# The first 17 and the last 4 microseconds of a fused attention and MLP kernel: transfers, LayerNorm and clock warm-up rearranged, last output tile cut in three

## Chip, cores, metric

One core of a Trainium2 chip. The metric is the device time of one execution in microseconds, taken over several executions. Six engines appear in the profile: PE (TensorE matmuls), PEld (its weight loads), DVE (VectorE), ACT (ScalarE), POOL (GpSimd), SP (SyncE, which here only issues transfers).

## The reference, cut to what matters

```python
mod = (silu(c) @ w_mod).reshape(1, 6, 1, 512)         # c: 512 values, w_mod: 512 x 3072
sa, ca, ga, sb, cb, gb = mod[:, 0], ..., mod[:, 5]
h = layernorm(x) * (1 + ca) + sa                      # x: 2048 x 512
x = x + ga * attention(h @ wq, k_cache[-512:], v_cache[-512:]) @ wo   # 32 heads of 128
h = layernorm(x) * (1 + cb) + sb
x = x + gb * (relu(h @ w1) @ w2)                      # 512 -> 1792 -> 512
```

All inputs and the output are bf16. Before the first query projection can run, four things must be there: the first 512 rows of x normalized and transposed, SiLU of c, its product with two sixths of w_mod (the "modulation columns"), and the first heads of wq.

## The kernel before

The rows of x are dealt so that partition p holds rows 16p to 16p+15; a tile is one row of each partition, and the first block of 512 rows is four tiles. The opening, in program order (cuts marked; `kb.op(engine, ...)` appends to that engine's stream and works out its semaphore waits from `reads` and `writes`):

```python
dma(c_col[:, :], c[0].rearrange("(c p) -> p c", p=P), "c", writes=[R_c], eng=ACT)
for t in range(TPB):                                   # TPB = 4 tiles
    dma(x_sb[:, t, :], xv[:, t, :], f"xa{t}", writes=[R_x[t]], eng=ACT if t % 2 else SP)
load_wm(1)                                             # two sixths of w_mod, SyncE queue
load_wm(0)
load_wq(0, 2); load_k(0); load_v(0); load_wq(2, 2)
# ... memsets, identity matrix, ScalarE's table ...
warm(48)                       # 48 matmuls of ident x ident, 128 columns, result unused
ln_stat(0); ln_stat(1); silu() # statistics on VectorE; silu: exp on ScalarE, rest on VectorE
ln_stat(2); ln_rstd(0, 0, 3); ln_stat(3); ln_rstd(0, 3, 4)   # power -0.5 on GpSimd
for tl in range(3):
    ln_norm(tl)                # VectorE
    ln_tposes(tl, [0, 2])      # four 128x128 transposes on TensorE into PSUM
for f in mod_cols_mm(0, QBK): f()   # 32 matmuls of one column
ln_norm(3); ln_tposes(3, [0, 2])
mod_cols_evac(0, QBK)
ln_mod_ps([0, 2], hT[0], R_hT[0], 1)   # scale and shift, two columns on DVE, two on ACT
# ...
q_mms(0); q_mms(1, 5)          # first query projections: 4 matmuls of 512 columns each
```

The end of each output tile (`y_group`): 14 matmuls of 512 columns, then two VectorE operations and a store.

```python
for fc in range(FC):           # FC = 14
    mm(bank[bk], h1T[b % 2][:, fc, tl*P:(tl+1)*P], w2_sb[:, fc, :], ...)
kb.op(DVE, lambda e: e.tensor_tensor(yt[i], bank[bk], gbf[:, :], op=ALU.mult), ...)
kb.op(DVE, lambda e: e.tensor_tensor(yo[i], yt[i], x_sb[:, t, :], op=ALU.add), ...)
dma(ov[:, t, :], yo[i], f"y{i}", reads=[R_yo[i]])
```

## Time and profile before

| | before |
|---|---|
| time, median of three (later four) executions | 568.4 us (568.33 of four, 567.71 to 568.82) |
| span of the profiled execution | 566.1 us |
| TensorE busy | 557.6 us, 98% |
| four tiles of x landed | 3.07, 5.28, 4.67, 6.95 us |
| modulation weights landed | 7.85 and 9.36 us |
| first query projection starts | 12.44 us |
| first exponential of scores starts | 16.88 us |
| last matmul ends, span ends | 562.43, 566.14 us |

Times inside an execution are microseconds from the span's start. A transfer has landed when its semaphore has its last count in the trace. The row to watch is the first exponential of scores: from there on the kernel is a steady pipeline that no part of the change touches. So "first exponential" measures the opening, and "last matmul to end of span" measures the end. The trace also records the clock that TensorE is granted: here it is 0.50 (half speed) from 9.85 to 16.68 us and 1.00 after. Below, "released" means that it goes to full speed, and it "falls" when it goes back to half. A "wide" matmul has 512 columns.

### The profile page before, as it was taken

What the parts mean: (1) busy time and instruction counts of PE and PEld (TensorE: products, weight loads), DVE (VectorE), ACT (ScalarE), POOL (GpSimd) and SP (SyncE); (2) the same over time, 40 slices, a digit from 0 to 9 for tenths busy, and PEclk for the clock granted to TensorE, in tenths of its full rate; (3) what the DMA queues carried; (4) which work ended last, traced back from release to release, by engine and by line L of the source; (5) the groups of instructions that cost most, each with busy time, mean ns of one, the idle gap of its engine ahead of it and who ended that gap; (6) DMA issues with size and microseconds to landing.
All of it is one profiled execution on the core that took longest, in us unless ns stands there. A gap on an engine that the chain in (4) does not pass through costs nothing.

```text
span 566.1 us, 9753 instructions
## 1 busy us (share of the span) xinstructions
PE 557.6 (98%) x4169; PEld 318.8 (56%) x4169; DVE 242.8 (43%) x532; ACT 347.5 (61%) x445; POOL 38.7 (7%) x41
## 2 busy tenths in 40 slices
PE   6999999999999999999999999999999999999997
PEld 5565555555565555555555555555555654444443
DVE  4344465533333655333346553333354448322133
ACT  2876666666666666666666666666666644432500
POOL 1000000002300000033000000330000000000000
PEclk8999999999999999999999999999999999999999
DMA  9785768342232147242522532121224210200001
GB/s 225 204 194 120 179 127 172 75 80 41 41 75 39 37 76 149 41 110 45 143 54 59 91 59 39 38 38 38 40 41 73 44 30 1 47 29 22 22 28 47
DMA packets 114340, 42.67 MB, mean 75 GB/s; under 512 B 94192, under 2 KB 113904, under 8 KB 114288
## 3 DMA queue, kind: packets, MB, share of 16 engines
q1 hardware_dynamic: 113472, 41.70, 35.1%
q8 instruction: 34, 0.56, 0.4%
q10 hardware_dynamic: 816, 0.26, 0.2%
q14 instruction: 18, 0.15, 0.1%
HBM read 18.35 MB, written 2.10 MB: 36 GB/s over the span
## 4 chain that ended last, share of the span: by engine, by line
PE 98%; DVE 1%; DMA 1%; issue 0%; ACTq 0%
PE psS L1351 28%; PE psO L1351 26%; PE psQ L1351 23%; PE psW L1351 20%; DMA x<-in_A_x_dram 1%; DVE st L1361 0%; PE psS L1354 0%; DVE PT L1632 0%; DVE PT L1633 0%; DVE mv L1362 0%; DVE hT L1398 0%; ACTq L1296 0%; DVE xn L1372 0%; DVE rstd L1366 0%; DVE tmp L1410 0%
## 5 line engine op out<-in xcount | busy, mean ns | idle before, releaser
L1465 ACT ACTIVATE PT<-psS 128x1024 bf16<-128x1024 f32 x256 | 262.7, 1028 | 129.6 <-PE psS L1351 129.6
L1351 PE MATMUL psS<-qT,kT 128*128 128x512 bf16 x512 | 152.2, 380 | 0.0
L1351 PEld LDWEIGHTS psO<-v,PT 128*128 128x128 bf16 x2048 | 126.6, 98 | 30.2
L1351 PE MATMUL psO<-v,PT 128*128 128x129 bf16 x2048 | 137.0, 220 | 0.0
L1351 PE MATMUL psQ<-hT,wq 128*128 128x512 bf16 x508 | 131.2, 381 | 0.8 <-DVE hT L1398 0.8
L1351 PE MATMUL psW<-wo,oT 128*128 128x512 bf16 x512 | 130.6, 379 | 0.0
L1475 DVE RECIPROCAL rinv<-psO 128x4 f32<-128x4 f32 x128 | 23.3, 182 | 234.9 <-PE psO L1351 234.9
L1476 DVE TENSOR_TENSOR o<-psO,rinv 128x512 bf16<-128x512 f32 x128 | 88.5, 691 | 4.7 <-DVE rinv L1475 0.3
L1351 PEld LDWEIGHTS psQ<-hT,wq 128*128 128x128 bf16 x508 | 49.8, 98 | 61.4 <-issue 1.5
L1351 PEld LDWEIGHTS psS<-qT,kT 128*128 128x128 bf16 x512 | 49.8, 98 | 59.5 <-ACT PT L1465 0.7
L1457 ACT ACTIVATE qT<-psQ 128x512 bf16<-128x512 f32 x127 | 75.2, 592 | 1.2 <-PE psQ L1351 1.2
L1621 ACT ACTIVATE wq<-psS 128x512 bf16<-128x512 f32 x56 | 33.4, 597 | 49.5 <-PE psS L1351 49.5
L1351 PEld LDWEIGHTS psW<-wo,oT 128*128 128x128 bf16 x512 | 45.0, 98 | 32.9 <-DVE acc L1498 1.2
L1498 DVE TENSOR_TENSOR acc<-psW,acc 128x512 f32<-128x512 f32 x48 | 33.1, 690 | 6.7 <-PE psW L1351 6.7
L1351 PE MATMUL psO<-wmw,wq 128*128 128x512 bf16 x140 | 31.2, 379 | 0.0
L1367 POOL TENSOR_TENSOR rstd<-rstd,cst 128x4 f32<-128x4 f32 (+2 forms) x9 | 8.7, 962 | 273.4 <-DVE rstd L1366 273.3
L1501 POOL TENSOR_TENSOR acc<-acc,gaf 128x512 f32<-128x512 f32 x12 | 15.3, 1271 | 168.7 <-DVE acc L1498 168.7
L1351 PE MATMUL psS<-h2T,wmw 128*128 128x512 bf16 x112 | 25.3, 379 | 0.0
L1351 PE MATMUL psS<-hT,wmw 128*128 128x512 bf16 x112 | 24.5, 379 | 0.0
L1632 DVE TENSOR_TENSOR PT<-psO,gbf 128x512 f32<-128x512 f32 x10 | 6.9, 691 | 40.2 <-PE psO L1351 40.2
L1361 DVE BATCH_NORM_STATS2 st<-x 128x6 f32<-128x512 bf16 x32 | 21.7, 679 | 4.4 <-DMA x<-in_A_x_dram 4.4
L1351 PEld LDWEIGHTS psO<-wmw,wq 128*128 128x128 bf16 x140 | 13.7, 98 | 16.5
(60 smaller groups left out, 168.9 us busy)
## 6 DMA issues: line engine op xcount, KB each, us to landing
wo<-in_A_wo_dram SPq DMA_DIRECT2D x4, 1024.0 KB, 6.1
wq<-in_A_wq_dram SPq DMA_DIRECT2D x7, 512.0 KB, 5.5
wmw<-in_B_w_dram SPq DMA_DIRECT2D x14, 256.0 KB, 3.1
wmw<-in_w_mod_dram SPq DMA_DIRECT2D x6, 512.0 KB, 5.5
oT<-o SPq DMA_TRANSPOSE x128, 2.4
out_dram<-PT SPq DMA_DIRECT2D x16, 128.0 KB, 1.8
x<-in_A_x_dram SPq DMA_DIRECT2D x3, 512.0 KB, 4.2
v<-in_A_v_cache_dram SPq DMA_DIRECT2D x8, 128.0 KB, 4.6
```

The costliest lines, as they stand in the source:

```text
L1351: kb.op(PE, lambda e: e.matmul(out_ap, lhsT, rhs, start=start, stop=stop), reads=reads, group_writes=[R_b[k] for k in bk], signal=signal)
L1361: kb.op(DVE, lambda e: e.bn_stats(st[:, t, :], x_sb[:, t, :]), reads=[R_x[t]], writes=[R_st[t]])
L1367: kb.op(POOL, lambda e: e.tensor_tensor(rstd[:, sl], rstd[:, sl], cst[:, 0:1].to_broadcast([P, hi - lo]), op=ALU.pow), reads=R_rstd[sl] + ...
L1457: kb.op(ACT, lambda e: e.activation(qT[u % NQT][:, :], bank[bk], ACTF.Copy), reads=[R_b[bk]], writes=[R_qT[u % NQT]])
L1465: kb.op(ACT, lambda e: e.activation(PT[u % NPT][:, pr * 2:pr * 2 + 2, :], s_ps[pr][:, :, :], ACTF.Exp, scale=scale), reads=[R_b[pr * 2], R ...
L1475: kb.op(DVE, lambda e: e.reciprocal(rinv[:, u, :], o_ps[:, :, P]), reads=[R_b[5], R_b[6]], writes=[R_rinv])
L1476: kb.op(DVE, lambda e: e.tensor_tensor(o_sb[u % NOS][:, :, :], o_ps[:, :, 0:P], rinv[:, u, :].unsqueeze(2).to_broadcast([P, TPB, P]), op=A ...
L1498: kb.op(DVE, lambda e: e.tensor_tensor(acc[:, tl, :], bank[WBK], acc[:, tl, :], op=ALU.add), reads=[R_b[WBK], R_acc[tl]], writes=[R_acc[tl]])
L1501: kb.op(eng, lambda e: e.tensor_tensor(acc[:, tl, :], acc[:, tl, :], gaf[:, :], op=ALU.mult), reads=[R_acc[tl], R_ga], writes=[R_acc[tl]])
L1621: kb.op(ACT, lambda e: e.activation(h1T[b % 2][:, fc, :], bank[bk], ACTF.Relu), reads=[R_b[bk]], writes=[R_h1[b % 2][fc]], pre=all_events( ...
L1632: kb.op(DVE, lambda e: e.tensor_tensor(yt[i], bank[bk], gbf[:, :], op=ALU.mult), reads=[R_b[bk], R_gb], writes=[R_yt[i]], pre=pt_done if c ...
```

## The change

The intent: get x, c and the modulation weights in faster, shorten VectorE's serial chain by giving one tile to ScalarE, keep TensorE's clock up through the first projections, and shorten what follows the last matmul. The core of the diff:

```diff
-    dma(c_col[:, :], c[0].rearrange("(c p) -> p c", p=P), "c", writes=[R_c], eng=ACT)
-    for t in range(TPB):
-        dma(x_sb[:, t, :], xv[:, t, :], f"xa{t}", writes=[R_x[t]], eng=ACT if t % 2 else SP)
-    load_wm(1)
-    load_wm(0)
-    load_wq(0, 2)
+    for i in range(2):                  # two transfers of 256 KB, rows of 2 KB
+        dma(x_sb[:, 2*i:2*i+2, :], xv[:, 2*i:2*i+2, :], f"xa{i}", ..., eng=ACT if i else SP)
+    dma(c_row[:, :], c[0].rearrange("(c p) -> c p", p=P), "c", writes=[R_c])   # 4 rows
+    load_wm01(0)                        # both sixths together: rows of 2 KB,
+    load_wm01(1, ACT)                   # half of the rows on each queue
+    load_wq(0, 2, ACT)
 # warm(n):
-            mm(bank[WBK][:, :P], ident[:, :], ident[:, :], ...)
+            mm(bank[WBK], ones[:, :], ones[:, 0:1].to_broadcast([P, QB]), ...)   # 512 columns
-    warm(48)
+    warm(7)
+    silu_exp(5)                         # c transposed on TensorE, exponential on ScalarE
+    warm(9)
+    # tile 3 on ScalarE: Copy with sum, Copy (-mean), Square with sum, Identity (+eps),
+    # after GpSimd's power: Copy (-mean*rstd), Identity with scale and bias
...
-    silu()
     ln_stat(2)
...
+    silu_mul(5)
     for tl in range(3):
         ln_norm(tl)
-        ln_tposes(tl, [0, 2])
-    for f in mod_cols_mm(0, QBK):
-        f()
-    ln_norm(3)
-    ln_tposes(3, [0, 2])
-    mod_cols_evac(0, QBK)
+    # first half of the modulation columns, transposes of tile 0, second half, copied out
+    for tl in range(1, TPB):
+        ln_tposes(tl, [0, 2])
+        warm(tl)                        # 1, 2, 3 wide matmuls
 # the last output tile:
+    mlp.pop()
+    mlp.extend(lambda a=a: y_group(NB - 1, TPB - 1, *a)
+               for a in ((0, D // 2, ACT), (D // 2, 3 * D // 4, SP), (3 * D // 4, D, ACT)))
```

With the last part go four output buffers in place of two.

More of the change, by code (lines that the diff above doesn't have):

```diff
@@ L1244, in build_fast @@
     wmw = T("wmw", [P, max(6 * DC * D, DC * F + FC * D)])
-    wm = [wmw[:, i * DC * D:(i + 1) * DC * D].rearrange("p (c n) -> p c n", c=DC) for i in range(6)]
+    wm01 = wmw[:, 0:2 * DC * D].rearrange("p (c n) -> p c n", c=DC)
+    wm = [wm01[:, :, 0:D], wm01[:, :, D:2 * D]] + [wmw[:, i * DC * D:(i + 1) * DC * D].rearrange("p (c n) -> p c n", c=DC) for i in range(2, 6)]
     w1_sb = wmw[:, 0:DC * F].rearrange("p (c f) -> p c f", c=DC)
@@ L1249, in build_fast @@
     xnT = T("xnT", [P, TPB, DC, P])
-    NY = 2
-    yt = [PT[0][:, :, :].rearrange("p a b -> p (a b)")[:, 2 * i * D:2 * (i + 1) * D].bitcast(F32) for i in range(NY)]
+    NY = 4
+    yt = [PT[i // 2 * 2][:, :, :].rearrange("p a b -> p (a b)")[:, 2 * (i % 2) * D:2 * (i % 2 + 1) * D].bitcast(F32) for i in range(NY)]
     yo = [PT[1][:, i, :] for i in range(NY)]
@@ L1254, in build_fast @@
     ones = T("ones", [P, P])
-    c_col = T("c_col", [P, DC])
+    c_row = T("c_row", [DC, P])
+    s3 = T("s3", [P, 4], F32)
     sc_bf = T("sc_bf", [P, DC])
@@ L1309, in build_fast @@
     R_st, R_mv, R_rstd = RL("st", NT), RL("mv", NT), RL("rstd", NT)
+    R_s3, R_eps = Res("s3"), Res("eps")
     R_rinv, R_vmax, R_chk, R_good, R_flag = Res("rinv"), Res("vmax"), Res("chk"), Res("good"), Res("flag")
@@ L1331, in load_v, with load_wm, load_wm01, wm_res @@
         dma(v_sb[:, g, :, 0:Dh], A_v_cache[0][g, Sk - W:, :].rearrange("(k p) d -> p k d", p=P), f"v{g}", writes=[R_v[g]], eng=eng)
-    def load_wm(sl, eng=None):
-        dma(wm[sl], w_mod[:, sl * D:(sl + 1) * D].rearrange("(c p) n -> p c n", p=P), f"wm{sl}", writes=[R_wm[sl]], eng=eng)
+    def load_wm(sl):
+        dma(wm[sl], w_mod[:, sl * D:(sl + 1) * D].rearrange("(c p) n -> p c n", p=P), f"wm{sl}", writes=[R_wm[sl]])
+    wm01v = w_mod[:, 0:2 * D].rearrange("(c p) n -> p c n", p=P)
+    def load_wm01(i, eng=None):
+        c0, c1 = i * DC // 2, (i + 1) * DC // 2
+        dma(wm01[:, c0:c1, :], wm01v[:, c0:c1, :], f"wm{i}", writes=[R_wm[i]], eng=eng)
+    def wm_res(sl, cc):
+        return R_wm[cc // (DC // 2)] if sl < 2 else R_wm[sl]
     def load_wo(j):
@@ L1357, in warm @@
         for i in range(n):
-            mm(bank[WBK][:, :P], ident[:, :], ident[:, :], True, True, [R_ident], [WBK], i == n - 1)
+            mm(bank[WBK], ones[:, :], ones[:, 0:1].to_broadcast([P, QB]), True, True, [R_ones], [WBK], i == n - 1)
     def ln_stat(t):
@@ L1405, in build_fast, with silu_exp, silu_mul @@
     QA = 2
-    def silu():
-        kb.op(ACT, lambda e: e.activation(tmp[:, :], c_col[:, :], ACTF.Exp, scale=-1.0), reads=[R_c], writes=[R_tmp])
+    def silu_exp(bk):
+        cT = bank[bk].bitcast(BF)[:, 0:DC]
+        kb.op(PE, lambda e: e.transpose(cT, c_row[:, :], ident[0:DC, 0:DC]), reads=[R_c, R_ident], group_writes=[R_b[bk]])
+        kb.op(ACT, lambda e: e.activation(tmp[:, :], cT, ACTF.Exp, scale=-1.0), reads=[R_b[bk]], writes=[R_tmp])
+    def silu_mul(bk):
+        cT = bank[bk].bitcast(BF)[:, 0:DC]
         kb.op(DVE, lambda e: e.tensor_scalar(tmp[:, :], tmp[:, :], 1.0, None, op0=ALU.add), reads=[R_tmp], writes=[R_tmp])
         kb.op(DVE, lambda e: e.reciprocal(tmp[:, :], tmp[:, :]), reads=[R_tmp], writes=[R_tmp])
-        kb.op(DVE, lambda e: e.tensor_tensor(sc_bf[:, :], c_col[:, :], tmp[:, :], op=ALU.mult), reads=[R_tmp, R_c], writes=[R_sc])
+        kb.op(DVE, lambda e: e.tensor_tensor(sc_bf[:, :], cT, tmp[:, :], op=ALU.mult), reads=[R_tmp, R_b[bk]], writes=[R_sc])
     def mod_cols_mm(which, bk):
@@ L1420, in mod_cols_mm @@
                         bank[bk][:, col:col + 1], wm[sl][:, cc, c2 * P:(c2 + 1) * P], sc_bf[:, cc:cc + 1],
-                        cc == 0, cc == DC - 1, [R_sc, R_wm[sl]], [bk], last))
+                        cc == 0, cc == DC - 1, [R_sc, wm_res(sl, cc)], [bk], last))
         return fs
@@ L1528, in add_ln @@
             add(s0 + TPB + 5 + cc // 2, lambda cc=cc: ln_mod_sb(cc, dst, r, which))
-    dma(c_col[:, :], c[0].rearrange("(c p) -> p c", p=P), "c", writes=[R_c], eng=ACT)
-    for t in range(TPB):
-        dma(x_sb[:, t, :], xv[:, t, :], f"xa{t}", writes=[R_x[t]], eng=ACT if t % 2 else SP)
-    load_wm(1)
-    load_wm(0)
-    load_wq(0, 2)
+    for i in range(2):
+        dma(x_sb[:, 2 * i:2 * i + 2, :], xv[:, 2 * i:2 * i + 2, :], f"xa{i}", writes=R_x[2 * i:2 * i + 2], eng=ACT if i else SP)
+    dma(c_row[:, :], c[0].rearrange("(c p) -> c p", p=P), "c", writes=[R_c])
@@ L1537, in build_fast @@
+    load_wm01(0)
+    load_wm01(1, ACT)
+    load_wq(0, 2, ACT)
+    load_wq(2, 2)
     load_k(0)
     load_v(0)
-    load_wq(2, 2)
     kb.op(POOL, lambda e: e.memset(ones[:, :], 1.0), writes=[R_ones])
+    kb.op(POOL, lambda e: e.memset(cst[:, 0:1], -0.5), writes=[R_cst])
     kb.op(POOL, lambda e: e.affine_select(ident[:, :], ones[:, :], pattern=[[1, P]], compare_op=ALU.is_equal, fill=0.0,
                                           base=0, channel_multiplier=-1), reads=[R_ones], writes=[R_ident])
-    kb.op(POOL, lambda e: e.memset(cst[:, 0:1], -0.5), writes=[R_cst])
+    kb.op(POOL, lambda e: e.memset(cst[:, 1:2], eps), writes=[R_eps])
@@ L1544, in build_fast @@
     kb.op(POOL, lambda e: e.memset(v_sb[:, :, :, P:VW], 1.0), writes=[R_v1])
     kb.op(ACT, lambda e: e.activation(cst[:, 2:3], cst[:, 0:1], ACTF.Exp), reads=[R_cst], writes=[Res("dummy")])
-    warm(48)
+    warm(7)
+    silu_exp(5)
+    warm(9)
+    t3 = TPB - 1
+    kb.op(ACT, lambda e: e.activation(xn[:, t3, :], x_sb[:, t3, :], ACTF.Copy, accum_out=s3[:, 0:1]), reads=[R_x[t3]], writes=[R_xn[t3], R_s3])
+    kb.op(ACT, lambda e: e.activation(s3[:, 1:2], s3[:, 0:1], ACTF.Copy, scale=-1.0 / D), reads=[R_s3], writes=[R_s3])
@@ new lines, in build_fast, with rstd_add @@
+    kb.op(ACT, lambda e: e.activation(xn[:, t3, :], x_sb[:, t3, :], ACTF.Square, bias=s3[:, 1:2], accum_out=s3[:, 2:3]), reads=[R_x[t3], R_s3], writes=[R_xn[t3], R_s3])
+    kb.op(ACT, lambda e: e.activation(rstd[:, t3:t3 + 1], s3[:, 2:3], ACTF.Identity, scale=1.0 / D, bias=cst[:, 1:2]), reads=[R_s3, R_eps], writes=[R_rstd[t3]])
+    def rstd_add(lo, hi):
+        kb.op(DVE, lambda e: e.tensor_scalar(rstd[:, lo:hi], mv[:, lo:hi, 1], eps, None, op0=ALU.add), reads=R_mv[lo:hi], writes=R_rstd[lo:hi])
@@ L1547, in build_fast, with rstd_pow @@
+    def rstd_pow(lo, hi):
+        kb.op(POOL, lambda e: e.tensor_tensor(rstd[:, lo:hi], rstd[:, lo:hi], cst[:, 0:1].to_broadcast([P, hi - lo]), op=ALU.pow),
+              reads=R_rstd[lo:hi] + [R_cst], writes=R_rstd[lo:hi])
     ln_stat(0)
     ln_stat(1)
-    silu()
+    rstd_add(0, 2)
+    rstd_pow(0, 2)
     ln_stat(2)
-    ln_rstd(0, 0, 3)
-    ln_stat(3)
-    ln_rstd(0, 3, 4)
+    rstd_add(2, 3)
+    rstd_pow(2, 4)
+    silu_mul(5)
     for tl in range(3):
         ln_norm(tl)
-        ln_tposes(tl, [0, 2])
@@ L1557, in build_fast @@
-    for f in mod_cols_mm(0, QBK):
-        f()
-    ln_norm(3)
-    ln_tposes(3, [0, 2])
-    mod_cols_evac(0, QBK)
+    kb.op(ACT, lambda e: e.activation(s3[:, 3:4], s3[:, 1:2], ACTF.Copy, scale=rstd[:, t3:t3 + 1]), reads=[R_s3, R_rstd[t3]], writes=[R_s3])
+    kb.op(ACT, lambda e: e.activation(xn[:, t3, :], x_sb[:, t3, :], ACTF.Identity, scale=rstd[:, t3:t3 + 1], bias=s3[:, 3:4]),
+          reads=[R_x[t3], R_rstd[t3], R_s3], writes=[R_xn[t3]])
+    fs = mod_cols_mm(0, QBK)
+    for f in fs[:len(fs) // 2]:
+        f()
@@ L1562, in build_fast @@
+    ln_tposes(0, [0, 2])
+    for f in fs[len(fs) // 2:]:
+        f()
+    mod_cols_evac(0, QBK)
+    for tl in range(1, TPB):
+        ln_tposes(tl, [0, 2])
+        warm(tl)
     ln_mod_ps([0, 2], hT[0], R_hT[0], 1)
@@ L1622, in h1_group, with y_group @@
               pre=all_events(R_wq) if b < 2 else ())
-    def y_group(b, tl):
-        pt_done = all_events(R_PT[0] + R_PT[1])
+    def y_group(b, tl, c0=0, c1=D, deng=None):
+        pt_done = all_events(R_PT[0] + R_PT[1] + R_PT[2])
         t = b * TPB + tl
@@ L1630, in y_group @@
         for fc in range(FC):
-            mm(bank[bk], h1T[b % 2][:, fc, tl * P:(tl + 1) * P], w2_sb[:, fc, :], fc == 0, fc == FC - 1, [R_h1[b % 2][fc], R_w2[fc]], [bk], fc == FC - 1)
-        kb.op(DVE, lambda e: e.tensor_tensor(yt[i], bank[bk], gbf[:, :], op=ALU.mult), reads=[R_b[bk], R_gb], writes=[R_yt[i]], pre=pt_done if cnt["y"] <= NY else ())
-        kb.op(DVE, lambda e: e.tensor_tensor(yo[i], yt[i], x_sb[:, t, :], op=ALU.add), reads=[R_yt[i], R_x[t]], writes=[R_yo[i]])
-        dma(ov[:, t, :], yo[i], f"y{i}", reads=[R_yo[i]])
+            mm(bank[bk][:, c0:c1], h1T[b % 2][:, fc, tl * P:(tl + 1) * P], w2_sb[:, fc, c0:c1], fc == 0, fc == FC - 1, [R_h1[b % 2][fc], R_w2[fc]], [bk], fc == FC - 1)
+        kb.op(DVE, lambda e: e.tensor_tensor(yt[i][:, c0:c1], bank[bk][:, c0:c1], gbf[:, c0:c1], op=ALU.mult), reads=[R_b[bk], R_gb], writes=[R_yt[i]],
+              pre=pt_done if cnt["y"] <= NY else ())
+        kb.op(DVE, lambda e: e.tensor_tensor(yo[i][:, c0:c1], yt[i][:, c0:c1], x_sb[:, t, c0:c1], op=ALU.add), reads=[R_yt[i], R_x[t]], writes=[R_yo[i]])
+        dma(ov[:, t, c0:c1], yo[i][:, c0:c1], f"y{i}", reads=[R_yo[i]], eng=deng)
     cut = {}
@@ L1652, in build_fast @@
                 mlp.extend(lambda n=n: cut_here(n) for n in ("dve", "sp", "pool"))
+    mlp.pop()
+    mlp.extend(lambda a=a: y_group(NB - 1, TPB - 1, *a) for a in ((0, D // 2, ACT), (D // 2, 3 * D // 4, SP), (3 * D // 4, D, ACT)))
     def pop_mlp(n):
```

## The prediction

> **What bounds the kernel now.** I read the page's busy shares and chain first, then the chain in order of time for the opening and for the end, then busy time by stretch for the clock, then the queues of the first microseconds.
>
> ```profile
> span 566.1 us, 9753 instructions
> ...
> PE 557.6 (98%) x4169; PEld 318.8 (56%) x4169; DVE 242.8 (43%) x532; ACT 347.5 (61%) x445; POOL 38.7 (7%) x41
> ...
> PE 98%; DVE 1%; DMA 1%; issue 0%; ACTq 0%
> ```
>
> TensorE is the bound and its chain fills the span. It is idle for 566.1 - 557.6 = 8.5 us in all, and none of the matmuls of the body is changed. So the change can only win in the first 17 us, before the pipeline of attention units runs, and after the last matmul. The first matmul that does work of the body is the query projection; this is how it is reached:
>
> ```profile
> 1.27 4.01 DMA x<-in_A_x_dram
> ...
> 5.30 0.70 DVE st L1361
> ...
> 7.53 0.17 DVE rstd L1366
> ...
> 8.70 0.42 DVE xn L1372
> ...
> 9.16 1.25 PE psS L1354 x12
> 10.41 0.83 PE psQ L1351 x32
> 11.24 0.46 PE psS L1354 x4
> ...
> 11.75 0.56 DVE hT L1398
> ...
> 12.44 1.86 PE psQ L1351 x4
> 14.31 1.71 PE psO L1351 x4
> 16.02 0.82 PE psS L1351 x2
> 16.84 0.86 PE psQ L1351 x4
> ```
>
> Columns: start, length, what. VectorE waits for the second tile of x until 5.28, then is serial until 8.70; transposes and modulation columns share TensorE until 11.7; the projections start at 12.44. The same four 512-wide projection matmuls take 1.86 and 1.71 us at 12.4 to 16.0 and 0.86 us at 16.84: half speed. The stretches show why:
>
> ```profile
> 1.40:6.44 5.04, 5.03 (x48) 5.03 (x48) 1.94 (x6) 1.69 (x3) 0.25 (x2) 1.00 0.65 187
> 6.44:9.85 3.41, 0.89 (x12) 0.50 (x11) 3.24 (x12) 0.00 (x0) 1.55 (x2) 1.00 1.31 301
> 9.85:16.67 6.82, 6.07 (x52) 3.11 (x52) 1.88 (x6) 2.64 (x4) 0.00 (x0) 0.50 1.15 305
> ```
>
> The columns are PE, PEld, DVE, ACT and POOL busy, granted clock, DMA share and GB/s. The clock is 0.50 from 9.85 to 16.67. The 48 warm-up matmuls of 128 columns end at 6.64; they ran at 5.23 us / 48 = 109 ns each, against 0.91 / 16 = 57 ns for the 129-column ones of the body, so they themselves were cold although the record says 1.00. They bought one fast stretch of 3.41 us, in which TensorE worked 0.89 us, and the clock fell just as real work began.
>
> ```profile
> q1 hardware_dynamic: 223, 0.21, 33.3%
> q10 hardware_dynamic: 530, 0.00, 14.0%
> ```
>
> These are the queues between 2 and 4 us: 530 packets that carry next to nothing on the ScalarE queue (it has 816 in the whole run: 512 elements of the vector c, 256 rows of 1 KB of x, 48 completions of three transfers). The two queues move 0.21 MB in 2 us, mean 105 GB/s, where the following microseconds reach 312 to 379. Tiles 1 and 3 of x stand behind those packets. At the end:
>
> ```profile
> 559.41 3.04 PE psQ L1351 x14
> ...
> 562.47 0.70 DVE PT L1632
> ...
> 563.19 0.69 DVE PT L1633
> ```
>
> After the last matmul there are 1.41 us of VectorE on a 512-wide tile and 566.1 - 563.88 = 2.2 us for the store.
>
> **What the Trainium skill says.** "TensorE: Matmul & The Clock Gate", Part 1: the clock is half by default, a window of 3413 ns of sustained work releases it, one idle window withdraws it, and the window runs free of the program. The trace agrees: the stretches last 3.41 and 2 x 3.41 us. Part 4 of the same page says that transposes do not count as busy in the same way; the 9.85 to 13.27 window, with transposes, one-column matmuls and about 0.8 us of projections, indeed did not release the clock. "DMA: Bandwidth & Descriptors", Rules for kernel authors: a non-contiguous last dimension becomes one descriptor per element, and issuing from several engines saves issue time only; the 530 packets agree with the first. "ScalarE: Activation LUTs", What ACT_TABLE_LOAD costs: an ACTIVATE is about 186 ns + 0.833 ns per column, about 93 ns more per pointer operand; the trace has 0.59 us for a 512-wide copy and 1.45 / 2 = 0.72 us for one with scale and bias pointers, which agrees. The page's Table sets section keeps cheap functions in every set; I take Square to be one and expect no second table load.
>
> **Opening, transfers.** c arrives as four rows of 256 B instead of 512 elements, and behind the first rows of x. x is two transfers of 256 KB, 2 KB rows, first on each queue, issued at 0.79. The first packet of x was moved at 1.8 us. Half a MB at an estimated 300 to 350 GB/s (from the 312 to 379 above) takes 1.5 to 1.7 us, plus some 0.3 us to the semaphore: both halves land at about 3.8 us. The first tile is thus later than before (3.10), the second much sooner (5.28).
>
> **Opening, LayerNorm.** VectorE from 3.8: two tiles of statistics at 0.93 us each (5.30 to 6.24 now) to 5.7, epsilon 0.17, third tile 0.93 to 6.8, epsilon, the three small SiLU operations 0.54 to 7.4, then three normalizations at 0.35 us (1.39 / 4) to 8.5. GpSimd's power, 0.84 us each, is at 6.8 and 7.75 and hides. ScalarE has tile 3: the SiLU exponential at about 4.4, a 0.61 us copy with the sum, a small one, a 0.70 us square, a small one, done near 6.4; after the second power 0.3 + 0.7 us, done near 8.8. Tile 3 was ready at 10.07 before. The 1 MB of modulation weights, third in line, should land near 7 (before: about 8.2), so they do not bind.
>
> **Opening, TensorE.** The modulation columns are now first: 16 matmuls of about 33 ns from 7.45, four transposes 0.3, 16 more 0.5, done at 8.9; then transposes 0.3, one warm matmul 0.22, 0.3, two 0.43, 0.3: last transpose at about 10.3 instead of 11.7. The three warm matmuls behind it (0.65) lie beside VectorE's and ScalarE's modulation, which needs 0.5 and 0.72 us before the first projection can start, at about 11.0, a gain of 1.4 us. The last of four modulated columns is ready 1.45 us after the start, at 11.9. With a full clock the first projection then ends at 12.15 and the second at 13.0 (4 x 0.216), the first score pair at 13.5, the first score exponential at about 13.8. Before it began at 16.88. So the gain is about **3.0 us** with the clock kept: 1.4 from the earlier start, 1.6 from the clock. From there on the first units are paced at 2.63 us by both TensorE and ScalarE (two exponentials of 1.03 and a copy of 0.59), later units by TensorE at 3.5, so the gain passes whole to the end.
>
> **The clock.** The wide matmuls start at about 1.05 and 16 of them are up to 16 x 0.427 = 6.8 us cold (half speed of 0.216): a full window is sure to lie in them. If it is released early they end at about 6.2, over a microsecond before the next work. From 7.45 on TensorE has little pause, but half of its work is one-column matmuls and transposes. I give 65% that the clock holds through the projections. If it falls, the gain is the earlier start and a little: 1.4 us. Mean: 0.65 x 3.0 + 0.35 x 1.4 = 2.4; I use 2.6, as the warm matmuls between the transposes are plainly there to hold it.
>
> **End.** Three pieces of 256, 128 and 128 columns: at 216 ns for 512 and 57 for 128 the estimate for 256 is 110, so 14 x (110 + 57 + 57) = 3.14 us instead of 3.02: 0.12 lost. VectorE on 512 takes 0.69,[...] 128 takes 0.29: two of them 0.61 instead of 1.41, 0.80 won; the earlier pieces (0.87 and 0.61 us) fit beside the next piece's 0.80 of matmuls or nearly so. The last store is 32 KB instead of 128, perhaps 0.2 us shorter, though its rows are 256 B. Net gain **0.8 us**.
>
> **Sum.** 2.6 + 0.8 = 3.4; 568.4 - 3.4 = 565.0. In the whole this is 0.6%.
>
> **Rivals.** (1) The clock falls anyway: gain 1.4 + 0.8 = 2.2, 566.2. For it: the 9.85 window fell with only 0.89 us of work before it. Against: warm matmuls fill the pause now. (2) ScalarE becomes the opening's bound: its small instructions wait on each other, the copy waits for the exponential, that for a transpose behind seven cold matmuls, and a second table load (1.28 us in this trace) would come twice. Then tile 3 is 1 to 2.5 us later and the sum of gains 1.5 to 2.5, 566 to 567. (3) The opening is bound by transfer, as the start-up rate, not the tiny packets, is what is slow: x would land near 5 and the modulation weights near 8.3, leaving the clock's and the end's gains, 2.4, 566.0. (4) All goes well, the transfers at 380 GB/s too: 563.9.
>
> **Range and chances.** The best case less a little and the rivals give 563.6 to 566.8. 2% is 11.4 us, more than the whole idle time of TensorE plus its cold stretch could return, so faster by over 2% has a chance of 0.01; slower would take a stall in the body, which is untouched: 0.01.
>
> **What would show it.** First statistics at 3.6 to 4.1; no tiny packets; one table load; last transpose near 10.3; first projection near 11.0; no 0.50 clock between 10 and 16; first score exponential near 13.8; last store issued 0.7 us after the last matmul. A half clock at 11 to 15, or a first score exponential later than 15.5, would prove the 3.0 wrong; a body whose length from the first score exponential to the last matmul differs from 562.45 - 16.88 = 545.6 by more than 0.5 us would prove wrong that the gain passes whole.

## The result

| | before | changed |
|---|---|---|
| median of four executions | 568.33 us | 564.1 us |
| range | 567.71 to 568.82 | 563.53 to 564.8 |
| span of the profiled execution | 566.1 | 562.5 |
| first exponential of scores | 16.88 | 14.10 |
| last matmul to end of span | 3.71 | 2.68 |

The ratio is 0.9927, 95% interval 0.9909 to 0.9944. Where a gain is given in microseconds below, it is (1 - ratio) x 568.3: here 4.1 us, interval 3.2 to 5.2. Experiments ran on three chips and in several jobs whose medians of the kernel before went from 567.94 to 568.95, so kernels of different jobs are compared by ratio and not by median.

The page of the changed kernel, its span, busy times and the chain's shares:

```profile
span 562.5 us, 9700 instructions
...
PE 553.7 (98%) x4097; PEld 316.9 (56%) x4172; DVE 242.2 (43%) x533; ACT 350.4 (62%) x453; POOL 38.7 (7%) x42
...
PE 97%; issue 1%; DMA 1%; DVE 1%
```

TensorE still bounds it. The chain in order of time, opening (start, length, what):

```profile
0.79 3.99 DMA x<-in_A_x_dram
...
4.80 0.70 DVE st L1373
...
7.55 0.15 DVE rstd L1574
...
8.25 0.55 PE psQ L1363 x16
...
10.54 0.22 PE psS L1366 x4
...
11.49 0.81 PE psQ L1363 x3
...
12.69 0.86 PE psO L1363 x4
...
14.06 0.86 PE psQ L1363 x4
```

The first statistics start at 4.80, hardly sooner than the second tile's did (5.30). The gain up to the first projection is 12.44 - 11.49 = 0.95 us. From the first projection to the first exponential it took 16.88 - 12.44 = 4.44 us and now takes 14.10 - 11.49 = 2.61: another 1.83, and four matmuls now take 0.86 us from the second head on. The clock in three of its windows (PE, PEld, DVE, ACT, POOL busy, granted clock, DMA share, GB/s):

```profile
3.31:6.72 3.41, 3.09 (x9) 0.84 (x7) 1.82 (x6) 2.24 (x8) 0.00 (x0) 1.00 1.04 376
6.72:10.14 3.42, 2.89 (x50) 1.97 (x50) 2.62 (x11) 1.48 (x4) 1.48 (x2) 1.00 1.30 249
10.14:13.55 3.41, 3.33 (x18) 1.32 (x17) 1.33 (x3) 2.04 (x3) 0.00 (x0) 1.00 1.15 321
```

The trace records the release at 6.72. The first row's 1.00 is only a filled-in value: before the first record no clock is known, and the wide matmuls ran at 0.427 us each there, half the speed of the body's. After that it holds; there is no stretch of 0.50. The queues between 2 and 4 us:

```profile
q10 hardware_dynamic: 181, 0.34, 51.8%
q1 hardware_dynamic: 130, 0.22, 35.6%
```

The ScalarE queue moves 0.34 MB with 181 packets where before 530 packets moved next to nothing. At the end, the chain:

```profile
558.28 1.58 PE psO L1363 x28
...
559.88 0.30 DVE PT L1673
...
560.21 0.29 DVE PT L1675
```

Between first exponential and last matmul lie 559.84 - 14.10 = 545.74 us, before 562.43 - 16.88 = 545.55: the body is unchanged to 0.2 us. The account of the two profiled executions closes: 2.78 us from the opening, 1.03 from the end, less 0.19, is 3.62, and 566.14 - 562.52 = 3.62. The two medians differ by 4.2; the profiled execution of before, 567.87 us, was faster than its median. Much of the scatter of the kernel before goes with the clock, as the next section shows.

### The profile page after: what moved, and what is told of

Read it like the earlier page. It is cut to its first block, busy times and chain, and to the rows that moved or that the text cites. A ratio compares the mean times of both kernels' runs of the same rounds, so it can differ in the third digit from the quotient of the medians.

```text
span 562.5 us, 9700 instructions
## 1 busy us (share of the span) xinstructions
PE 553.7 (98%) x4097; PEld 316.9 (56%) x4172; DVE 242.2 (43%) x533; ACT 350.4 (62%) x453; POOL 38.7 (7%) x42
## 4 chain that ended last, share of the span: by engine, by line
PE 97%; issue 1%; DMA 1%; DVE 1%
PE psS L1363 28%; PE psO L1363 26%; PE psQ L1363 23%; PE psW L1363 20%; DMA x<-in_A_x_dram 1%; DVE st L1373 0%; PE psS L1366 0%; DVE mv L1374 0%; DVE rstd L1574 0%; DVE PT L1673 0%; DVE PT L1675 0%; DVE tmp L1427 0%; DVE sc_bf L1428 0%; DVE tmp L1426 0%
## 5 line engine op out<-in xcount | busy, mean ns | idle before, releaser
L1363 PE MATMUL psW<-wo,oT 128*128 128x512 bf16 x451 | 117.9, 379 | 3.2
L1363 PE MATMUL psO<-wmw,wq 128*128 128x512 bf16 (+1 forms) x164 | 32.7, 352 | 0.3
L1379 POOL TENSOR_TENSOR rstd<-rstd,cst 128x4 f32<-128x4 f32 x7 | 7.1, 1012 | 265.3 <-DVE rstd L1378 265.3
L1673 DVE TENSOR_TENSOR PT<-psO,gbf 128x512 f32<-128x512 f32 (+1 forms) x12 | 7.5, 624 | 40.4 <-PE psO L1363 40.4
L1363 PEld LDWEIGHTS psO<-wmw,wq 128*128 128x128 bf16 x168 | 15.4, 98 | 16.5
```

The lines of the kernel that those rows point to most:

```text
L1363: kb.op(PE, lambda e: e.matmul(out_ap, lhsT, rhs, start=start, stop=stop), reads=reads, group_writes=[R_b[k] for k in bk], signal=signal)
L1379: kb.op(POOL, lambda e: e.tensor_tensor(rstd[:, sl], rstd[:, sl], cst[:, 0:1].to_broadcast([P, hi - lo]), op=ALU.pow), reads=R_rstd[sl] + ...
L1673: kb.op(DVE, lambda e: e.tensor_tensor(yt[i][:, c0:c1], bank[bk][:, c0:c1], gbf[:, c0:c1], op=ALU.mult), reads=[R_b[bk], R_gb], writes=[R_ ...
```

## Experiments

Theory: the parts add up; the end is worth about 1 us, the kept clock about 1.6, and an earlier first projection the rest. Rivals: the clock costs nothing because projections wait for data; the transfers' row size, or c's packets, or VectorE's chain alone make the opening. Twelve kernels ran, all correct. The table holds what the traces of their profiled executions show; each is then told.

| run | ratio (95%) | gain us | x landed | weights landed | first projection | first exponential |
|---|---|---|---|---|---|---|
| changed kernel | 0.9927 (0.9909 to 0.9944) | 4.1 | 4.98 | 7.95 | 11.49 | 14.10 |
| tail_only | 0.998 (0.9967 to 0.9992) | 1.1 | 7.18 | 9.18 | 12.22* | 16.68 |
| open_only | 0.9945 (0.9932 to 0.9957) | 3.1 | 5.02 | 8.00 | 12.18 | 14.79 |
| no_warm | 0.9959 (0.9944 to 0.9974) | 2.3 | 4.85 | 7.83 | 11.60* | 16.06 |
| before_long_warm | 0.9982 (0.9966 to 0.9998) | 1.0 | 7.00 | 9.35 | 12.47* | 16.93 |
| no_warm_between | 0.9912 (0.9897 to 0.9926) | 5.0 | 4.92 | 7.86 | 11.73* | 14.34 |
| c_column | 0.9998 (0.9984 to 1.0011) | 0.1 | 7.89 | 10.32 | 14.85 | 17.46 |
| before_c_row | 0.9994 (0.998 to 1.0007) | 0.3 | 4.41 | 9.37 | 11.77* | 15.55 |
| x_rows_1k | 0.9937 (0.992 to 0.9954) | 3.6 | 5.09 | 9.93 | 13.30 | 15.91 |
| tile3_vector | 0.9934 (0.9921 to 0.9948) | 3.8 | 4.84 | 7.80 | 12.19 | 14.79 |
| improved_a | 0.9977 (0.996 to 0.9994) | 1.3 | 6.39 | 8.75 | 12.21 | 14.81 |
| improved_b | 0.9978 (0.9966 to 0.9991) | 1.3 | 5.95 | 8.85 | 13.80 | 16.41 |
| unbroken_warm | 0.9916 (0.9903 to 0.993) | 4.8 | 5.00 | 8.00 | 10.95 | 13.56 |

"Landed" is the last of the transfers concerned. (*) The trace lacks the record of the first projection's first matmul; the number is the start of its weight load plus 0.03 us, the distance in the two kernels' own traces.

The record also gives the mean granted clock of every execution, not only of the profiled one. A window of 3.41 us at half speed takes 0.003 from the mean over 566 us, so 0.994 means two such windows (the 6.82 us of the kernel before) and 0.991 three. In the job of tail_only the kernel before ran eleven times: the eight executions at 0.991 took 568.74 us on average, the three at 0.994 took 567.88. A mean of 1.000 says only that no half-speed stretch was recorded; what comes before the first record counts as full (no_warm has 1.000 though its clock was first released at 17.14). The kernel before was at 0.991 in 8 of 11 executions of one job (chip 6) and in 1 of 11 of another (chip 0); by the difference above, an estimate, that alone moves a gain by some 0.5 us, so gains of different jobs are not comparable more closely than that.

### tail_only and open_only: do the two ends add?

```diff
 # tail_only: the kernel before, plus
+    mlp.pop()
+    mlp.extend(... three pieces ...)     # and the four output buffers
 # open_only: the changed kernel, without those lines
```

> The kernel before with only the last output tile in three column pieces. Theory (the parts add): the opening is as before, and the time from the last matmul to the end falls from 3.7 us to about 2.6 us while the last tile's matmuls grow by 0.1 us: 0.9 to 1.0 us faster than before, about 567.4. Rival (the gain is in the opening and the store's latency covers the end): under 0.3 us faster.

> The changed kernel with its last tile whole again. Theory: 0.9 to 1.0 us slower than the changed kernel, 2.7 to 3.2 us faster than before. First score exponential at about 14.1 us as in the changed kernel. If the whole 4.2 us between the medians comes from the opening, it is over 3.5 us faster than before.

tail_only gained 1.1 us (median 567.34), open_only 3.1 us (565.52). The sum, 4.2, is the whole gain of 4.1: they add. In tail_only's trace 2.68 us lie between last matmul and end, as in the changed kernel, and 3.77 in open_only, as in the one before. The expectation that open_only's first exponential stays at 14.1 failed: it came at 14.79. Its trace explains that: the clock was released at 9.45, not 6.72, so the sixteen warm matmuls lasted until 8.81 and kept the modulation columns waiting, whose input had been ready at about 8.2. The two kernels have the same opening, so the difference is one between executions; the wait for c, which landed at 4.84 here and at 4.48 there, differed too.

### no_warm: what the clock is worth

```diff
-    warm(7)
     silu_exp(5)
-    warm(9)
...
-        warm(tl)
```

> The changed kernel with no warm-up matmuls at all. Theory (a kept clock is worth 1.6 us in the opening): the clock stays at half until one whole window of projections and scores has passed, near 16 us or later; modulated columns start at about 11 us as before, the first score exponential near 15.8 instead of 14.1, and the kernel is 1.5 to 2.5 us slower than the changed one. Rival (the opening is set by waits for data, and warm matmuls in front of it only delay): within 0.5 us of the changed kernel.

The gain over the kernel before fell from 4.1 to 2.3 us, so the warm-up is worth about 1.8 us, within the expected 1.5 to 2.5 (the two runs are of different jobs, and their intervals just touch). Two lines of its timeline:

```profile
13.26 1.91 PE L1363 MATMUL psO<-hT,wq 128*128 128x512 bf16 x4
...
16.06 1.02 ACT L1482 ACTIVATE PT<-psS 128x1024 bf16<-128x1024 f32 x1 [0.26 <-PE psS L1363]
```

The four matmuls of the second head take 1.91 us, as in the kernel before, where the changed one shows 1.03 in the same view; the trace first records a released clock at 17.14. The first projection starts only 0.1 us later than in the changed kernel (11.60 against 11.49), the first exponential 1.96 later: nearly all of the loss lies behind the first projection, where the half clock is. So the rival, that warm matmuls in front only delay, is out.

### before_long_warm: the clock alone, in the kernel before

```diff
-            mm(bank[WBK][:, :P], ident[:, :], ident[:, :], ...)
+            mm(bank[WBK], ones[:, :], ones[:, 0:1].to_broadcast([P, QB]), ...)
-    warm(48)
+    warm(24)
```

> The kernel before with 24 wide warm-up matmuls in place of 48 narrow ones, reaching to about 9 us, nothing else. Theory (the clock alone is worth about 1.6 us): no half clock between 10 and 16 us, first score exponential near 15.3 instead of 16.9, about 1.6 us faster than before. Rival (the first projections wait for modulated columns, not for TensorE's rate): under 0.6 us faster though the clock holds.

This did not do what it was meant to. The clock was released at 4.38, held for two windows, and fell at 11.21; the profiled execution gained nothing. The two windows:

```profile
4.38:7.79 3.41, 3.41 (x17) 1.46 (x15) 2.06 (x7) 0.13 (x1) 0.00 (x0) 1.00 0.97 326
7.79:11.21 3.42, 2.03 (x48) 1.57 (x47) 2.48 (x8) 0.00 (x0) 1.55 (x2) 1.00 1.32 247
```

In the second window TensorE was busy 2.03 of 3.42 us, all but the first quarter microsecond of it with transposes and one-column matmuls, and that was not enough. The granted clock of the six executions sorts them: three at 0.994 took 568.42 to 568.68 us, two at 0.997 took 567.38 and 567.09, and the one at 1.000 took 565.85. So within this kernel each half-speed window less goes with some 1.3 us, and the execution without any on record was 2.7 us faster than those with two. That is one execution and a reading after the fact, but it points the same way as no_warm. The run shows that warming longer before the opening's small work does not suffice to hold the clock reliably.

### no_warm_between: who holds the clock

```diff
         ln_tposes(tl, [0, 2])
-        warm(tl)
```

> The changed kernel without the 1, 2 and 3 wide matmuls between the last transposes. Theory A (the 16 wide matmuls before are enough to hold the clock until the projections): the last transposes come 0.35 to 0.65 us earlier, no half clock, so 0.3 to 0.6 us faster than the changed kernel. Theory B (the matmuls between are what holds the clock): the clock falls to 0.5 near 10 us and the kernel is 1 to 1.6 us slower than the changed one.

Theory A in its verdict: no fall, and a gain of 5.0 instead of 4.1 us (median 563.59; the intervals overlap, and the jobs differ). Not in its detail: in the profiled execution the last transposes were not earlier, because the clock was released only at 10.32. Two windows, one on the way to the release and the one after it:

```profile
3.49:6.91 3.42, 2.82 (x8) 0.83 (x7) 2.06 (x6) 2.03 (x8) 0.17 (x1) 1.00 1.05 372
...
10.32:13.73 3.41, 2.46 (x20) 1.25 (x19) 1.57 (x5) 2.05 (x3) 0.00 (x0) 1.00 1.16 321
```

The first has a pause of 0.6 us while TensorE waits for c between the 7th and the 8th warm matmul. 2.82 us of work in it did not release the clock; 3.09 us in the changed kernel's window, with a pause of 0.3, did. The windows are set by their own phase, and c landed at 4.48, 4.77 or 4.84 us in the profiles of the changed kernel, this run and open_only; so an execution gets its release near 6 or near 10 us by chance. That is a weakness of the change: the wait for c stands in the middle of its warm-up.

### c_column and before_c_row: the tiny packets

```diff
 # c_column: the changed kernel with
+    dma(c_row[:, :], c[0].rearrange("(c p) -> p c", p=P), ..., eng=ACT)   # first; c_row is 128 x 4
     for i in range(2): ...
-    dma(c_row[:, :], c[0].rearrange("(c p) -> c p", p=P), ...)
 # before_c_row: the kernel before with
-    dma(c_col[:, :], c[0].rearrange("(c p) -> p c", p=P), ..., eng=ACT)
     for t in range(TPB): ...
+    dma(c_row[:, :], c[0].rearrange("(c p) -> c p", p=P), ...)
-    warm(48); ...; silu()
+    warm(30); silu_exp(5); warm(18); ...; silu_mul(5)
```

> The changed kernel, with the vector c fetched as before, one packet for each element and first on the ScalarE queue. Theory (the tiny packets hold up the rows of x): x lands 1 us or more later than 4.8, and all that follows with it, so 0.7 to 1.3 us slower than the changed kernel. Rival (the landing at 4.8 is set by something else, since c as four rows did not make x land at 3.8 as predicted): first statistics within 0.3 us of 4.8, and within 0.4 us in all.

> The kernel before with one change: the vector c comes as four rows behind the first tile of x and is transposed on TensorE among the warm-up matmuls. Theory (the 512 tiny packets are what the opening's transfers lose): tiles 1 and 3 of x land near 3.7 and 5.1 instead of 5.28 and 6.95, the statistics start and end 1 us or more earlier, and the kernel is 0.7 to 1.6 us faster than before although the clock still falls. Rival (the gain needs the 2 KB rows and the new order of work): under 0.4 us faster.

c_column lost the whole gain: ratio 0.9998, some 4.0 us slower than the changed kernel where 0.7 to 1.3 was expected. The mechanism was the theory's, the size was not. The ScalarE queue's row between 2 and 4 us, and two lines of the timeline:

```profile
q10 hardware_dynamic: 283, 0.00, 7.4%
```

```profile
7.91 0.69 DVE L1373 BATCH_NORM_STATS2 st<-x 128x6 f32<-128x512 bf16 x1 [1.93 <-DMA x<-in_A_x_dram]
...
10.37 0.50 PE L1363 MATMUL psQ<-sc_bf,wmw 128*128 128x1 bf16 x14 [0.61 <-DMA wmw<-in_w_mod_dram]
```

Half of x and half of the weights stand behind the 512 packets on that queue: x is there at 7.89, the weights at 10.32, and both VectorE and TensorE wait for them. While TensorE waited, the clock fell at 10.97, and all five executions have 0.994 or 0.997, so the 4 us contain the lost clock. What costs 4 us is thus not the packets alone but the packets with so much behind them: the kernel before had only two tiles of x there.

before_c_row is the counterpart, and it disappointed: 0.3 us with an interval of -0.4 to 1.1, not 0.7 to 1.6. Its x landed by 4.41 instead of 6.95, and VectorE finished its statistics a microsecond sooner, as the theory says. The modulation columns started at 9.53 instead of 10.21, directly behind the transposes of three tiles, and the first projection at 11.77 instead of 12.44. The weights, still on one queue, had landed at 9.37: they did not bind, but by 0.16 us only. The profiled execution, the fastest of the six at 566.29, gained 1.33 us up to the first exponential, half of it before the first projection; the other half lies behind it, where its clock was released at 14.57 instead of 16.68. The clock explains much of the disappointment: the two executions at 0.991 took 568.25 and 568.53, the three at 0.994 took 566.29 to 567.49, on average 1.2 us less than the eight executions of the kernel before at 0.994 in the same job (566.75 against 567.93); one at 1.000 took 567.49. So at an equal clock c as rows gained about what the theory says; but three executions sorted after the fact show this only weakly.

### x_rows_1k: the size of the rows of x

```diff
-    for i in range(2):
-        dma(x_sb[:, 2*i:2*i+2, :], xv[:, 2*i:2*i+2, :], f"xa{i}", ..., eng=ACT if i else SP)
+    for t in range(TPB):
+        dma(x_sb[:, t, :], xv[:, t, :], f"xa{t}", writes=[R_x[t]], eng=ACT if t % 2 else SP)
```

> The changed kernel, with the first block of x fetched by four transfers of 1 KB rows, alternating between the queues as before, instead of two of 2 KB rows. Theory A (2 KB rows issued at once are a gain): the later tiles land after 4.8 us, VectorE's statistics end later, 0.3 to 0.8 us slower. Theory B (what the large transfers lose is the early first tile, and c's packets were the trouble): the first tile lands near 3.2, the statistics of three tiles end 0.6 to 1.2 us earlier than 7.5, and the kernel is 0.3 to 0.8 us faster, until the modulation weights bind.

Inconclusive on the time: 3.6 us gained against 4.1, the intervals overlap. The first tile did land sooner, at 3.54, and the statistics of three tiles ended at 6.28 instead of 7.52, as theory B says. Yet the profiled execution was slow:

```profile
10.07 0.54 PE L1363 MATMUL psQ<-sc_bf,wmw 128*128 128x1 bf16 x16 [0.61 <-DMA wmw<-in_w_mod_dram]
```

The weights came at 9.93: a last few dozen of their packets trickled in between 7 and 9.4 us while the other transfers had moved on. This execution, 566.48 us, was the slowest of five (563.81 to 566.48). Whether 1 KB rows cause that straggling, or it was this execution's chance, is open. The 2 KB rows are not shown to be a gain.

### tile3_vector: the fourth tile back on VectorE

```diff
-    # tile 3 on ScalarE (six operations)
     ln_stat(2)
+    ln_stat(3)
-    rstd_add(2, 3)
+    rstd_add(2, 4)
...
-    for tl in range(3):
+    for tl in range(4):
         ln_norm(tl)
```

> The changed kernel with the fourth tile's LayerNorm on VectorE again. Theory (VectorE's serial chain is the opening's path): its statistics put 0.9 us before SiLU, the modulation columns start near 9.2 instead of 8.25, and the kernel is 0.8 to 1.1 us slower than the changed one. Rival (the modulation weights or TensorE's queue set the path): under 0.4 us.

First exponential 14.79, 0.69 later than in the changed kernel; input of the modulation columns ready 0.68 later (8.87 against 8.19). In the time, 3.8 against 4.1 us gained, it cannot be told from noise. But this execution does not show that VectorE's chain made the difference, for the warm-up ended just as late. From its chain:

```profile
5.08 3.95 PE psW L1363 x9
```

The nine wide matmuls behind c ran at half speed until about 8.9 (the chain has them to 9.04), as they did in open_only, which has ScalarE's tile and the same first exponential, 14.79. In the changed kernel, with its release at 6.72, the chain did run through VectorE (4.80 to 8.20, its lines under "The result"). So ScalarE's tile is worth at most about 0.7 us, when the warm-up ends early, and this run does not show that it is worth anything.

### improved_a, improved_b: an attempt that failed

```diff
+    dma(c_row[:, :], c[0].rearrange("(c p) -> c p", p=P), "c", writes=[R_c], eng=ACT)   # first
     for i in range(2): ...      # improved_b: four transfers of 1 KB rows
-    load_wq(0, 2, ACT)
+    load_wq(0, 2)
-    warm(7); silu_exp(5); warm(9)
+    warm(5); silu_exp(5); warm(10)
+    silu_mul(5)                 # ahead of the statistics
# fourth tile normalized on VectorE from ScalarE's sums; all modulation columns ahead of the
# transposes, copied out by ScalarE; one warm matmul between transposes
```

> A version meant to beat the changed kernel: c as rows first on the ScalarE queue so that SiLU is done before x lands; the modulation columns right after the warm-up, ahead of all transposes, copied out by ScalarE; the fourth tile normalized by VectorE from ScalarE's sums; projection weights only on the SyncE queue; one warm matmul between transposes. If the path in the changed kernel is SiLU, modulation columns and the two waits of warm matmuls before the last transposes, the modulated columns start near 9.8 instead of 10.8 and the kernel is 0.6 to 1.2 us faster than the changed one (ratio to before near 0.991). If the modulation weights bind (landing after 8), 0 to 0.4 us.

> The same as the last, with x in four transfers of 1 KB rows. If the statistics can start at 3.6 instead of 4.8 and the modulation weights do not bind, another 0.3 to 0.6 us faster. If 1 KB rows delay the weights behind them, as in the one look at that variant (9.9 us instead of 8.0), 0.5 us or more slower than the last.

Both gained only 1.3 us over the kernel before. improved_a's timeline names one reason:

```profile
8.79 0.90 PE L1363 MATMUL psQ<-sc_bf,wmw 128*128 128x1 bf16 x30 [2.28 <-DMA wmw<-in_w_mod_dram]
```

The first two matmuls of the modulation columns had run at 6.3; the other thirty waited 2.28 us for the half of the weights on the ScalarE queue. With c put first there, its four small rows moved at 1.74, but the half of x behind them, issued at 1.38, sent its first packet at 3.61 and landed at 6.39, against 4.98 in the changed kernel, and everything behind it was late as well. Why that packet came so late is open: in improved_b, with the same four rows ahead, the first packet of x on that queue came at 2.79. Idle TensorE also loses the clock: improved_b's fell at 9.32, after a window with 1.51 us of work, and all five of its executions have 0.993 or 0.997. improved_a kept it in the profiled execution, 564.95 us; its six executions are two at 1.000 (564.89 and 564.95), two at 0.997 (566.23 and 566.93) and two at 0.994 (567.32 and 568.13). So most of what improved_a lacks on average goes with the clock, and the order of transfers made TensorE wait. I had optimized the engines' order and worsened the order of transfers, which binds.

### unbroken_warm: repair the weak spot only

```diff
-    warm(7)
-    silu_exp(5)
-    warm(9)
+    warm(12)
+    silu_tpose(5)      # the transposition of c alone, c has long landed
+    warm(8)
 # ScalarE: the exponential of c after the fourth tile's square
...
         ln_tposes(tl, [0, 2])
-        warm(tl)
+    warm(3)            # behind the last transposes only
```

> The changed kernel with the wait for c moved out of the first warm-up matmuls (12 wide ones, the transposition of c, 8 more, no pause), ScalarE's exponential behind the fourth tile's square, and no warm matmuls between transposes, only the 3 behind the last. Theory (a pause of 0.3 to 0.9 us in the warm-up decides by chance of the clock's window whether the clock is released near 6 or near 10 us, and the 1 and 2 matmuls between are pure delay): release before 8 us, no fall, last transposes near 10.0, first score exponential at 13.5 to 13.8 instead of 14.1 to 14.8, 0.4 to 1.0 us faster than the changed kernel, ratio to before 0.990 to 0.992. Rival (without the matmuls between, the clock falls near 11): 0.5 us or more slower than the changed kernel.

First exponential at 13.56, as expected:

```profile
13.56 1.02 ACT L1485 ACTIVATE PT<-psS 128x1024 bf16<-128x1024 f32 x1
```

The clock was released at 5.51 and did not fall. The five executions lie between 563.32 and 563.68, a spread of 0.36 us where the changed kernel's four have 1.27: which fits that with an unbroken warm-up of 6 us and more the window's phase no longer matters much. Median 563.63, gain 4.8 us over the kernel before (interval 4.0 to 5.5). It beats the kernel before; against the changed kernel it is 0.6 us ahead by ratio, but the intervals overlap and the two never ran in one job, so I do not call that shown.

## Why the prediction was right

The measured 564.1 lies in the range 563.6 to 566.8, 0.9 under the predicted 565.0. By its own steps:

- **TensorE bounds it and only the two ends can win**: right. The body stayed at 545.6 to 545.7 us, and 0.7% is the whole gain.
- **x lands at about 3.8**: wrong by a microsecond, 4.78 and 4.98. The step took the full rate from the first packet on. The queues moved 35 GB/s between 1 and 2 us, 221 between 2 and 3, 343 between 3 and 4, and of the sixteen counts of each half's semaphore the eighth came at 3.92 and 4.13, the last 0.85 us later. This was the first half of rival 3.
- **The weights land near 7 and do not bind**: 7.95 instead, and 9.36, not 8.2, in the kernel before: the packets' start times had been read as the landing. They just did not bind, as their input was ready at 8.19. c_column, improved_a and x_rows_1k show that they are the next bound at once when they are later.
- **LayerNorm**: 2.73 us for three tiles' statistics and epsilon where 3.0 was reckoned; SiLU done at 8.19 instead of 7.4, all from the late x; tile 3 at 9.72 instead of 8.8. One table load, as assumed. The prediction read 0.72 us for an operation with two pointers as agreeing with its rule; by that rule it is 186 + 427 + 2 x 93 ns = 0.80 us, and the fourth tile's took 0.81.
- **TensorE up to the first projection**: last transpose done 10.76 instead of 10.3, first projection 11.49 instead of 11.0. From 8.25 to 10.76 is 2.51 us, where 2.85 was reckoned. So of the microsecond lost on x only half was left here, and 0.3 at the first exponential (14.10 for 13.8). Gain of the opening 2.78 us; 3.0 was named for a kept clock and 2.6 used, a little over the mean of the chances, 2.4. The step to 14.10 is partly luck of opposite errors: x was 1.0 late, VectorE up to SiLU 0.2 shorter, TensorE up to the last transpose 0.34 shorter, and the way from the first projection to the first exponential 0.2 shorter (2.61 for 2.8).
- **The clock is worth 1.6 and holds with 65%**: it held in both profiled executions of this opening (changed kernel and open_only), and all nine on record have a mean clock of 0.999 or more; no_warm puts its worth at 1.8 to 2.0. What the prediction had not seen is that the release itself comes at different times: 6.72 in the changed kernel's profiled execution, 9.45 in open_only's. "A full window is sure to lie in" the sixteen matmuls was wrong, since they are not without a pause: the wait for c lies in the middle. And the window from 9.85 to 13.27, read as agreeing with what the skill says of transposes, shows nothing about them: it had some 2.7 us of work, and open_only's window from 2.62 to 6.04, with 2.75 us of it nearly all in wide matmuls, did not release the clock either.
- **The end, 0.8**: 1.03 less 0.07 for the longer last tile, 0.96. VectorE's part went from 1.44 to 0.64 and the store's from 2.25 to 2.02, both as worked out; the matmuls of the three pieces took 3.11 us (3.14 predicted).
- **Which part makes it**: the prediction priced c's packets only through x. c_column shows that without c as rows the rest of the opening is worth less than nothing (0.1 us gained in all, of which the end alone is 1.1), the lost clock included. That is the largest thing the working had too small. ScalarE's tile and the 2 KB rows of x are not shown to gain, and no run separates the two queues of the weights from their 2 KB rows.
- **Sum**: 2.6 + 0.8 = 3.4 predicted; 3.62 between the profiled executions, 4.1 by ratio. The rest would fit the clock: the profiled execution of the kernel before had two half-speed windows, and executions with three took some 0.9 us longer. For the four executions of the kernel before in the result no clock is on record, so this is not shown.

## What to carry to other kernels

In an opening, look for the order in which transfers land before the order of work on the engines: a vector fetched element by element, with half of the other transfers behind it, or a weight half put behind the wrong thing, cost some 3 to 4 us here, the clock lost through the waiting included, and reordering the engines around it did not make up for it. With little behind it, in the kernel before, the same vector cost 0.3 us by ratio and about 1 at an equal clock. A warm-up has to be dense and without waits, and the first long matmuls have to follow before TensorE has been mostly idle, or busy only with transposes and one-column matmuls, for a window of 3.4 us. When a kernel's executions scatter by a microsecond, read the granted clock of every execution before crediting an edit, and compare executions of equal clock.

## What the Trainium skill lacked or had wrong

- "TensorE: Matmul & The Clock Gate", Part 1, speaks of a busy and of an idle window without shares. In windows of 3.41 us here, 2.91 us of work (tail_only, 3.80 to 7.21) and more released the clock, and 2.75 and less did not; of two windows near 2.8 one did (before_c_row, 11.16 to 14.57, with its missing matmul added) and one did not (no_warm_between, 3.49 to 6.91, 2.82). It was kept with 1.91 us (improved_a, 4.59 to 8.00) and more, and fell with 1.59 (before_c_row, 4.33 to 7.74) and less. The exception is the window of before_long_warm with 2.03 us, nearly all transposes and one-column matmuls, which fell; that agrees with what Part 4 says of transposes, and adds the one-column matmuls as suspects.
- "DMA: Bandwidth & Descriptors", Rules for kernel authors, says that a non-contiguous last dimension becomes one descriptor per element, but gives no time. Here 512 packets of 2 bytes took from 2.83 to 5.29 us on their queue (c_column), and the core's queues moved 33 and 74 GB/s in the two full microseconds of that.
- The same page says that issuing from several engines saves issue time only. The weights landed at 7.95 us from two queues and at 9.37 from one (before_c_row); rows of 2 KB against 1 KB differ as well, and so does what stands ahead, so this is no proof against it. But what a transfer costs those behind it in its queue, microseconds here (c_column: x at 7.89 instead of 4.98), has no figure on the page. Nor is it plain: with four rows of 256 B ahead, the first packet of x came 2.2 us after its issue in improved_a and 1.4 in improved_b, where 1.2 is seen without them.
- "ScalarE: Activation LUTs" gives the cost of an ACTIVATE, but not that one with a sum is followed by an instruction of its own that reads the accumulator: 0.19 us each, twice in the fourth tile's chain.
